# Sparse attention into a split-precision MLP: weight fetches of the first combined chunk, PSUM rotation and the transposition of the probabilities

## The chip, the cores and the metric

The kernel runs on one core of one Trainium2 chip. The metric is the device time of one execution in microseconds. Before the change three runs gave a median of 704.69 us (702.12 to 708.5).

## What is computed

```python
k_sum, v_sum = max and mean of k, v over blocks of 32 keys          # (4, 8, 24, 64)
scores = [q.k/8 where |i-j| < 16 else -1e9,  q.k_sum/8 + log 32]
a = softmax(scores);  attn = a @ [v, v_sum]                         # q, k, v: (4, 8, 768, 64)
x = attn, heads side by side                                        # (3072, 512)
out = ((x @ w_a) * (x @ w_b)) @ w_out      # w_a, w_b: (512, 1536), w_out: (1536, 512)
```

Everything is 32-bit float.

## The kernel before

Each number is held as a high and a low part, and a product is three matmuls (high by high, high by low, low by high). The hidden dimension is cut into 12 blocks of 128, numbered `f`; a block has one tile of `w_a`, one of `w_b` and one of `w_out`, all 36 kept in SBUF (`homes`). The 24 groups of 128 tokens are cut into eight chunks `u`: four chunks of two groups, then from `PLAIN = 4` on four chunks of four groups (512 tokens).

Chunks 0 to 3 use the weights as they are (`item`, matmuls at L1358 and L1429). Chunks 4 to 7 use combined weights (`fast`): seven products of half size instead of eight, from the block's two own tiles (number 0, and half of number 3) and from two sums and differences of them (numbers 1 and 2). `combine` makes these for all 12 blocks while chunks 2 and 3 run: it adds the parts (L1277), subtracts in halves (L1285), splits the results into high and low (L1296 and L1297), and writes all four tiles to a buffer in HBM, `store`, through SP's DMA queue. In `fast` each of 48 items (chunk by block) reads its four tiles back with `fetch` (L1492, `t<-combined` in the profile), into one of two rings of four tiles that alternate. The freed homes of the weights serve as rings, as the chunk's inputs (`XTILES`, two sets) and as gates (`GATES`, the homes of block 11).

An item of `fast` is seven products of six matmuls each (L1522), into the two halves of the PSUM banks `h0` and `h1`; ScalarE copies the first out (L1534) and VectorE adds the others into `acc` in SBUF (L1536, L1539, L1542, L1544). The two results are multiplied on GpSimd (L1550; in chunk 7 on VectorE), cast by ScalarE (L1552), the low part is subtracted on GpSimd (L1555), and twelve matmuls with `w_out` follow (L1562).

Beside all this runs the attention of the chunks to come, one group of 128 tokens at a time. Scores (L855) go to the banks `c0` and `c1`, one for each half of the heads; VectorE scales and masks them (L875) and takes the maximum (L883), ScalarE the exponentials (L912), GpSimd divides (L938). The probabilities are turned by twelve VectorE transpositions per group (L983), each 32 partitions by eight pieces of 32 columns, which place each block directly. Then come the products with the values (L999) in `c0`, and ScalarE copies these to `S0` (L1010). When a chunk's four groups are there, `mix` makes the seven combined inputs: subtractions on VectorE (L1332), high parts on ScalarE (L1327), low parts on GpSimd (L1328). `prep_values` sums blocks of `v` on GpSimd (L778) at a new batch.

Every instruction is put into a list with a rank, and `Work.emit` writes the program. A table `ORDER` gives the order of each of the five engines (SP's is that of the DMA issues) word for word; an engine never leaves that order.

Of the kernel before, what the change touches and what calls it, by code (L numbers as in the profile page):

```python
# [333 lines left out]
def attention_moe(  # L334
# [10 lines left out]
    nc = tc.nc  # L345
# [26 lines left out]
    COPIES = ("AA", "AA", "AA", "AA")  # L372
    MEANS = "DPP"
    TURNS = 5
    FILL = 2

    const = ctx.enter_context(tc.tile_pool(name="const", bufs=1))
    wp = ctx.enter_context(tc.tile_pool(name="weights", bufs=1))
# [1285 lines left out]
```

## Time and profile before

| | before |
|---|---|
| median of three runs | 704.69 us |
| the profiled execution, own time | 701.9 us |
| its span, first to last instruction | 700.2 us |
| granted TensorE clock, mean | 0.978 of full speed |
| busy: TensorE matmul / weight load | 641.7 / 571.7 us |
| busy: VectorE / GpSimd / ScalarE | 498.2 / 361.6 / 252.5 us |
| moved by DMA | 164.92 MB, 236 GB/s on the average |

All durations come from the one profiled execution. Busy times of TensorE include time in which a matmul waits in the array's pipeline, since the ends of matmuls are modelled; how fast it streams is read from stretches in which nothing holds it up. The stages used below are: chunks 0 to 3 up to 267.4 us, then the combined chunks 4, 5, 6 and 7, which start at 267.4, 391.6, 498.9 and 597.5 us with their first matmul at L1522.

### The profile page before, as it was taken

The page shows a single profiled execution, that of the slowest core. Times are in us where ns is not written, and L with a number is a line of the kernel's source. Part 1 is how long each engine was busy: PE and PEld are TensorE (multiplying, and loading weights), DVE is VectorE, ACT ScalarE, POOL GpSimd, SP SyncE. Part 2 cuts the span into 40 slices and gives each one's busy share as a digit, 9 for nine tenths or more (in the row PEclk, how much of TensorE's full clock was granted, in tenths as well). Part 3 has the DMA queues.
Part 4 walks back from the last instruction along what each step waited for, and adds up shares of the span by engine and source line. Part 5 has one row for each costly group of instructions (what it writes and reads, how often), then busy time and mean ns, then how long its engine had stood idle before and what let it go on. Part 6 is the DMA issues. An engine that isn't in the chain of part 4 may idle for free.

```text
span 700.2 us, 14435 instructions
## 1 busy us (share of the span) xinstructions
PE 641.7 (92%) x5316; PEld 571.7 (82%) x5316; DVE 498.2 (71%) x974; ACT 252.5 (36%) x706; POOL 361.6 (52%) x386
## 2 busy tenths in 40 slices
PE   7899999997998988889988989899999999999995
PEld 5699877786987867778877878789899989989995
DVE  4877899975899968636787988688876643444442
ACT  4887866331445423321323401515142121111111
POOL 6773555642678669677357643445635455211110
PEclk9899999999999999999998999999999999999998
DMA  9999944255779888988988887878967867678661
GB/s 248 285 277 277 320 87 96 65 144 151 239 236 310 252 283 256 299 243 266 324 235 239 244 234 233 276 232 258 291 200 267 283 232 252 204 283 300 239 200 60
DMA packets 186911, 164.92 MB, mean 236 GB/s; under 512 B 136264, under 2 KB 148808, under 8 KB 186840
## 3 DMA queue, kind: packets, MB, share of 16 engines
q1 hardware_dynamic: 186696, 163.86, 78.4%
q8 instruction: 42, 0.69, 0.4%
q14 instruction: 29, 0.24, 0.1%
q10 hardware_dynamic: 144, 0.13, 0.1%
HBM read 135.20 MB, written 28.31 MB: 234 GB/s over the span
## 4 chain that ended last, share of the span: by engine, by line
PE 45%; DVE 19%; DMA 17%; POOL 6%; SPq 6%; issue 4%; ACT 2%; DVEq 0%; ACTq 0%; POOLq 0%
PE h L1522 20%; PE o L1562 11%; DMA t<-combined 9%; PE h L1358 6%; SPq L529 5%; DVE pt L983 4%; PE o L1429 3%; DMA S<-in_v_dram 3%; PE c L999 2%; DVE S L1332 2%; DMA combined<-t 2%; POOL S L778 2%; DVE S L1285 2%; DVE c L595 1%; SPq L1492 1%
## 5 line engine op out<-in xcount | busy, mean ns | idle before, releaser
L1522 PEld LDWEIGHTS h<-x,t 128*128 128x128 f32 x2016 | 249.6, 194 | 42.2 <-issue 8.4
L1522 PE MATMUL h<-x,t 128*128 128x256 f32 x2016 | 260.2, 280 | 24.5 <-DMA t<-combined 11.5
L1562 PE MATMUL o<-w,gate 128*128 128x512 f32 x576 | 149.2, 385 | 1.7 <-POOL gate L1555 1.7
L1358 PE MATMUL h<-x,w 128*128 128x256 f32 (+1 forms) x792 | 135.0, 327 | 4.9 <-DVE gh L1420 4.6
L1358 PEld LDWEIGHTS h<-x,w 128*128 128x128 f32 x792 | 118.5, 192 | 17.7 <-DVE gh L1420 6.1
L1562 PEld LDWEIGHTS o<-w,gate 128*128 128x128 f32 x576 | 100.2, 193 | 11.7 <-POOL gate L1555 2.1
L1555 POOL TENSOR_TENSOR gate<-g,gate 128x512 fp32r<-128x512 f32 x47 | 61.0, 1298 | 90.9 <-ACT gate L1552 90.6
L1550 POOL TENSOR_TENSOR g<-sums 128x512 f32<-128x512 f32 x36 | 47.6, 1321 | 89.8 <-DVE sums L1544 78.7
L1536 DVE TENSOR_TENSOR sums<-h,sums 128x512 f32<-128x512 f32 x48 | 33.1, 689 | 77.2 <-PE h L1522 68.2
L1534 ACT COPY sums<-h 128x256 f32<-128x256 f32 x48 | 17.8, 371 | 149.1 <-PE h L1522 129.7
L983 DVE STREAM_TRANSPOSE pt<-s 32x256 f32<-32x256 f32 x144 | 62.7, 435 | 4.4 <-POOL s L938 1.8
L1552 ACT CAST gate<-g 128x512 fp32r<-128x512 f32 x48 | 29.7, 619 | 90.5 <-POOL g L1550 41.6
L1544 DVE TENSOR_TENSOR sums<-h,sums 128x512 f32<-128x512 f32 x48 | 33.0, 688 | 31.5 <-PE h L1522 30.6
L912 ACT ACTIVATE s<-s,nml 128x120 f32<-128x120 f32 x112 | 43.1, 387 | 33.6 <-DVE nml L883 33.5
L778 POOL TENSOR_TENSOR S<-S 96x512 f32<-96x512 f32 (+3 forms) x42 | 32.2, 767 | 29.7 <-DMA S<-in_v_dram 27.8
L1429 PE MATMUL o<-w,last 128*128 128x512 f32 x174 | 43.8, 388 | 0.7 <-ACT last L1417 0.6
L938 POOL TENSOR_TENSOR s<-s,nml 128x480 f32<-128x480 f32 x32 | 32.0, 1008 | 23.3 <-DVE nml L934 16.8
L1328 POOL TENSOR_TENSOR x<-S,x 128x512 fp32r<-128x512 f32 x28 | 37.8, 1356 | 5.1 <-ACT x L1327 4.9
L611 POOL TENSOR_TENSOR w<-S,w 128x512 fp32r<-128x512 f32 x24 | 30.6, 1282 | 18.6 <-ACT w L608 14.6
L1429 PEld LDWEIGHTS o<-w,last 128*128 128x128 f32 x174 | 31.8, 190 | 6.6 <-ACT last L1417 2.3
L1542 DVE TENSOR_TENSOR sums<-h,sums 128x512 f32<-128x512 f32 x48 | 33.0, 687 | 4.4 <-PE h L1522 3.3
L1297 POOL TENSOR_TENSOR t<-S,t 128x512 fp32r<-128x512 f32 x24 | 30.9, 1296 | 7.3 <-ACT t L1296 7.3
(153 smaller groups left out, 863.0 us busy)
## 6 DMA issues: line engine op xcount, KB each, us to landing
t<-combined SPq DMA_DIRECT2D x144, 512.0 KB
combined<-t SPq DMA_DIRECT2D x24, 512.0 KB
t<-combined SPq DMA_DIRECT2D x48, 256.0 KB
raw<-in_moe_w_a_dram SPq DMA_DIRECT2D x12, 512.0 KB
raw<-in_moe_w_b_dram SPq DMA_DIRECT2D x12, 512.0 KB
raw<-in_moe_w_out_dram SPq DMA_DIRECT2D x12, 512.0 KB
combined<-w SPq DMA_DIRECT2D x12, 512.0 KB
out_dram<-S SPq DMA_DIRECT2D x23, 256.0 KB
```

The costliest lines, as they stand in the source:

```text
L529: lambda: nc.sync.dma_start(out=out, in_=in_), rate=rate,
L778: lambda: nc.gpsimd.tensor_tensor(out=out, in0=i0, in1=i1, op=ALU.add),
L912: lambda h=h, c=c, more=more: nc.scalar.activation(y[h][:, c, :], x[h][:, c, :], AF.Exp, bias=m[:, 0, h, c : c + 1], scale=1.0, **more,),
L983: lambda js=js, qs=qs, rs=rs: nc.vector.transpose(out=pv[js, rs, qs], in_=sv[qs, rs, js]),
L1328: pool(rank, 1.24, [f"S0.{i}", hk], [lk], lambda: nc.gpsimd.tensor_tensor(out=half(1), in0=raw(i), in1=half(0).bitcast(F32), op=ALU.subtract))
L1358: nc.tensor.matmul(ps, w[:, c, part, :], xin[xpart][:, :, c].rearrange("p g (a b) -> p g b a", a=2), start=(i == 0), stop=(i == n - 1),)
L1429: nc.tensor.matmul(bank[ok[j]], (gh if first else gl)[:, j * P : (j + 1) * P], w[:, :, part, :].rearrange("p (z a) n -> p z n a", a=2), st ...
L1522: nc.tensor.matmul(ps, w[:, c, part, :], x[:, xpart, c].rearrange("p g (a b) -> p g b a", a=2), start=m == 0, stop=m == 5,)
L1536: dve(CHAIN, 0.65, ["h1", "h1R", rk], [f"{ak}.0", f"{ak}.1"], lambda: nc.vector.tensor_tensor(out=acc(0, 2), in0=h1, in1=acc(5).broadcast_ ...
L1550: lambda eng=nc.gpsimd if slow else nc.vector: eng.tensor_tensor(out=g, in0=acc(0, 5)[:, 0:4:3], in1=acc(0, 5)[:, 2:5:2], op=ALU.mult))
L1555: lambda eng=nc.gpsimd if n < n1 - 1 else nc.vector: eng.tensor_tensor(out=gate(i, 1), in0=gt, in1=gate(i, 0).bitcast(F32), op=ALU.subtract),
L1562: nc.tensor.matmul(bank[f"o{j}"], gate(i, z)[:, j * P : (j + 1) * P], w[:, :, part, :].rearrange("p (z a) n -> p z n a", a=2), start=f == ...
```

## The change

- Blocks 8 to 11 (`HELD`) are no longer combined during chunks 2 and 3. In chunk 4 their own two tiles are read from their homes, and tiles 1 and 2 are made in the ring just before use (`combine(f, r)`); all four are still written to `store` for the later chunks. Chunk 4 takes the blocks in the order 0, 8, 1, 9, 2, 10, 3, 11, 4, 5, 6, 7 (`TURN_OF`).
- Odd chunks take that order backwards, and a chunk's first two items use what the last two of the chunk before left in the rings: no fetch. The tiles change their places: gates go to block 4's homes, the second set of inputs mostly to the held blocks' homes, and tile 3 of both rings shares one home.
- The last two products of an item go to `c1`; which half of `h0` a product takes alternates by item. The sum is written in `c1`, and the multiplication (now on VectorE in all chunks) reads it there.
- Scores of chunks 5 to 7 use `c0` alone: two half steps, one after the other, and the values after them.
- Probabilities from chunk 3 on: one VectorE transposition of all 128 partitions (chunks 3 and 4: two, of half the columns) into a scratch tile, then 12 (24) ScalarE copies of 32 partitions put the blocks where they belong.
- In `mix` the subtractions move from VectorE to GpSimd, but for chunk 4, where they stay on VectorE and everything is done in two halves. In chunk 4's attention a second buffer lets the next group's scores begin before the present group's transposition. Copies of finished outputs (`finish`, to `S1`) go to ScalarE, except for the last chunk's.
- `ORDER` is written anew for all engines.

The diff without the table, cut to its core:

```diff
-        pe(-1, 1.06, [qk] + (near if masked else KT), banks, fn)
+        split = banks[0] == banks[1]
+        if not split:
+            pe(-1, 1.06, [qk] + (near if masked else KT), banks, fn)
         x = [bank[n].rearrange("p (c x) -> p c x", x=P)[:, :, :COLS] for n in banks]
...
+            if split:
+                pe(-1, 0.53, [qk] + KT, banks[:1], lambda h=h: fn((h,)))
...
+        for rows in (slice(0, 8),) if u > PLAIN else (slice(0, 4), slice(4, 8)):
+            n = rows.stop - rows.start
+            tk = ["turn"] if n == 8 else [f"kin0.{r}" for r in range(0, P, 32)]
+
+            def turn_room(n=n):
+                x = kin[:, : 4 * P]
+                if n == 8:
+                    if not turning:
+                        turning.append(wp.tile([P, 8 * P], F32, tag="last", name="turning"))
+                    x = turning[0]
+                return x.rearrange("p (n x) -> p n x", x=P)
+
+            dve(
+                rank, 0.71 if n == 4 else 1.3, sk if n == 8 else [sk[rows.start // 4]], tk,
+                lambda rows=rows, turn_room=turn_room: nc.vector.transpose(out=turn_room(), in_=sv[:, rows, :]),
+            )
+            for i, j in pairs_ij:
+                qs, js = slice(32 * i, 32 * (i + 1)), slice(32 * j, 32 * (j + 1))
+                act(
+                    rank, 0.13 + n * 32 / 1030, tk + ["S0.2"] * own, [f"{key}{i}{j}"],
+                    lambda js=js, qs=qs, rows=rows, turn_room=turn_room: nc.scalar.copy(
+                        out=pv[js, rows, qs], in_=turn_room()[qs, :, js]
+                    ),
+                )
...
-        banks = ["c0", "c1"]
+        banks = ["c0", "c1" if u <= PLAIN else "c0"]
...
-                if i + 1 < n and not after and u > PLAIN:
+                if i + 1 < n and not after:
                     begin(i + 1)
                 bring(i)
                 turned(i)
-                if i + 1 < n and u == PLAIN:
-                    begin(i + 1)
...
     AT = [3 * f + x for f in range(NF) for x in range(2)]
-    XTILES = (AT[:7], AT[15:22])
-    RING = (AT[7:11], AT[11:15])
-    GATES = AT[22:24]
+    HELD = (8, 9, 10, 11)
+    TURN_OF = (0, 8, 1, 9, 2, 10, 3, 11, 4, 5, 6, 7)
+    XTILES = (AT[1:8], AT[17:24])
+    RING = (AT[10:13] + AT[:1], AT[13:16] + AT[:1])
+    GATES = AT[8:10]
     store = dram.tile([NF, 4, P, 1024], I32, name="combined")
...
+        base = 0 if ring is not None else f % 2 * 2
+        first, second_ = f"S1.{base}", f"S1.{base + 1}"
+        rank = MIX + 0.001 * f
+        end = [] if ring is not None else [f"end{f}"]
...
-            (((2, 0), (1, 0), (1, 2)), ALU.add), (((2, 2), (0, 0), (1, 0)), ALU.subtract),
-            (((3, 0), (1, 2), (2, 2)), ALU.subtract), (((3, 2), (0, 2), (3, 0)), ALU.subtract),
+            (((0, 0), (0, 0), (1, 0)), ALU.subtract), (((1, 0), (1, 0), (1, 2)), ALU.add),
+            (((1, 2), (1, 2), (0, 0)), ALU.subtract), (((0, 2), (0, 2), (1, 2)), ALU.subtract),
         ):
-            (pool if o[0] == 3 else dve)(
-                MIX, 0.72 if o[0] == 3 else 0.36, [f"S1.{i}" for i in {x[0], y[0]} - {o[0]}], [f"S1.{o[0]}"],
-                lambda o=o, x=x, y=y, op=op, eng=nc.gpsimd if o[0] == 3 else nc.vector: eng.tensor_tensor(
+            eng = (dve, nc.vector) if o[1] == 0 else (pool, nc.gpsimd)
+            eng[0](
+                rank, 0.78, [f"S1.{base + i}" for i in {x[0], y[0]} - {o[0]}], [f"S1.{base + o[0]}"],
+                lambda o=o, x=x, y=y, op=op, eng=eng[1]: eng.tensor_tensor(
                     out=room(*o, 2), in0=room(*x, 2), in1=room(*y, 2), op=op),
...
+        for j, x, home in ((1, 1, a), (2, 0, b)):
+            i = home if ring is None else RING[ring][j]
+            keys, key = tile_keys(i), f"S1.{base + x}"
...
+        apart = u == PLAIN
+        cuts = [slice(g, g + 1) for g in range(G)] if apart else [slice(0, G)]
...
+        def less(o, x, y, gs):
+            (dve if apart else pool)(
+                rank, 0.78 if apart else 1.31, [named(f"S0.{i}", gs) for i in (x, y) if i != o], [named(f"S0.{o}", gs)],
+                lambda eng=nc.vector if apart else nc.gpsimd: eng.tensor_tensor(
...
-            copy, eng = ((nc.scalar.copy, act), (nc.vector.tensor_copy, dve))[j % 2]
+            copy, eng = ((nc.scalar.copy, act), (nc.vector.tensor_copy, dve))[j % 2 if end or space == "S0" else 0]
...
     ORDERED = (
-        (0, (0, 0), 0, "h0", 0), (1, (0, 1), 1, "h1", 0.1), (5, (2, 0), 5, "h1R", 0.15),
-        (6, (1, 1), 6, "h0R", 0.25), (4, (1, 0), 4, "h0", 0.3), (3, (3, 0), 3, "h1", 0.4),
-        (2, (2, 1), 2, "h1R", 0.45),
+        (0, (0, 0), 0, 0, 0), (1, (0, 1), 1, "h1", 0.1), (5, (1, 1), 5, "h1R", 0.15),
+        (6, (2, 0), 6, 1, 0.25), (4, (1, 0), 4, 0, 0.3), (3, (3, 0), 3, "c1", 0.4),
+        (2, (2, 1), 2, "c1R", 0.45),
     )
...
+        own = ("h0", "h0R") if i == 0 else ("h0R", "h0")
+
+        def product(j, y, k, hk):
+            if u == PLAIN and f in HELD and j in (0, 3):
+                w, y_ = homes[3 * f + j // 3], y + j // 3
+            else:
+                w, y_ = rings[RING[r][j]], y + (j == 3) * r
+            w = w[:, 2 * y_ : 2 * y_ + 2]
             x = x_tile(s, k)
...
-        dve(CHAIN, 0.65, ["h1", "h1R"], [f"{ak}.2", f"{ak}.3"], lambda: nc.vector.tensor_tensor(
-            out=acc(2, 2), in0=h1, in1=acc(2, 2), op=ALU.add))
+        dve(CHAIN, 0.69, [f"{ak}.2", f"{ak}.3"], ["c1", "c1R"], lambda: nc.vector.tensor_tensor(
+            out=c1, in0=c1, in1=acc(2, 2), op=ALU.add))
-        slow = n < n1 - NF
-        (pool if slow else dve)(
-            CHAIN, 1.24 if slow else 0.65, [f"{ak}.{x}" for x in (0, 2, 3, 4)], ["g0", "g1"],
-            lambda eng=nc.gpsimd if slow else nc.vector: eng.tensor_tensor(
-                out=g, in0=acc(0, 5)[:, 0:4:3], in1=acc(0, 5)[:, 2:5:2], op=ALU.mult))
+        dve(CHAIN, 0.69, ["c1", "c1R", f"{ak}.0", f"{ak}.4"], ["g0", "g1"], lambda: nc.vector.tensor_tensor(
+            out=g, in0=c1, in1=acc(0, 5)[:, 0:5:4], op=ALU.mult))
...
-        elif (3 in us) and f < NF:
-            combine(f)
+        elif 3 in us:
+            if f not in HELD:
+                combine(f)
...
-        u, f = PLAIN + (n - n0) // NF, (n - n0) % NF
+        u, z = PLAIN + (n - n0) // NF, (n - n0) % NF
+        f = TURN_OF[NF - 1 - z if u % 2 else z]
+        r = (z + u) % 2
         if n == n0:
             next(attention(u + 1))
-        if f == 0 and u < NU - 1:
+        if z == (8 if u == PLAIN else 0) and u < NU - 1:
             mix(u + 1)
-        if f == 7 and u < NU - 2:
+        if z == (8 if u == PLAIN else 7) and u < NU - 2:
             next(attention(u + 2))
-        fetch(n, f)
-        fast(n, u, f, n0, n1)
+        if u == PLAIN and f in HELD:
+            combine(f, r)
+        elif u == PLAIN or z > 1:
+            fetch(f, r)
+        fast(n, u, z, f, r, n0, n1)
```

## Rows read from the trace of the kernel before

**Rows 1.** Windows by stage: each engine's busy us, then clock, DMA share, GB/s.
```profile
160.00:267.40 107.40, 97.96 (x766) 83.94 (x766) 90.33 (x174) 43.53 (x125) 69.23 (x65) 0.97 0.81 248
267.40:391.60 124.20, 105.86 (x945) 95.05 (x946) 88.12 (x171) 37.01 (x123) 80.86 (x86) 0.95 0.91 266
391.60:498.90 107.30, 98.85 (x900) 89.67 (x898) 89.56 (x190) 32.97 (x115) 55.70 (x53) 1.00 0.86 252
498.90:597.50 98.60, 96.20 (x845) 89.45 (x844) 57.18 (x110) 24.41 (x70) 44.70 (x36) 1.00 0.75 248
```

**Rows 2.** Groups of TensorE instructions by line and shape: count, busy us, mean ns, idle before.
```profile
L1522 PE MATMUL h<-x,t 128*128 128x256 f32 x2016 | 260.2, 280 | 24.5 <-DMA t<-combined 11.5 <-DVE sums L1536 2.6 <-DVE sums L1542 2.1
L1562 PE MATMUL o<-w,gate 128*128 128x512 f32 x576 | 149.2, 385 | 1.7 <-POOL gate L1555 1.7
```

**Rows 3.** Chain that ended last, stretches where TensorE streams: start us, us, what.
```profile
331.73 1.05 PE c L855 x32
...
415.13 1.08 PE c L999 x32
...
548.34 2.59 PE o L1562 x12
...
637.87 3.35 PE h L1522 x30
```

**Rows 4.** The same chain inside the first combined chunk.
```profile
309.97 5.56 DMA S<-in_v_dram
...
335.25 7.00 DMA combined<-t
343.18 8.12 DMA t<-combined
```

**Rows 5.** Timeline of ScalarE at the first combined item.
```profile
288.89 0.62 ACT L1552 CAST gate<-g 128x512 fp32r<-128x512 f32 x1 [1.69 <-DMA combined<-t]
```

**Rows 6.** TensorE's waits from 160 to 267 us: releaser, total us, times, longest.
```profile
PE c L999 <- DMA vw<-S: 4.3, 1, 4.3
PE h L1358 <- DVE gh L1420: 3.8, 2, 2.7
```

**Rows 7.** Groups of VectorE instructions by line and shape.
```profile
L983 DVE STREAM_TRANSPOSE pt<-s 32x256 f32<-32x256 f32 x144 | 62.7, 435 | 4.4 <-POOL s L938 1.8
L1536 DVE TENSOR_TENSOR sums<-h,sums 128x512 f32<-128x512 f32 x48 | 33.1, 689 | 77.2 <-PE h L1522 68.2 <-POOL g L1550 3.5 <-POOL x L1328 2.7
...
L1332 DVE TENSOR_TENSOR S<-S 128x512 f32<-128x512 f32 x16 | 21.9, 1371 | 2.6 <-ACT S L1010 2.3
...
L875 DVE SCALAR_TENSOR_TENSOR s<-c,mask 128x480 f32<-128x480 f32 x28 | 17.7, 646 | 4.9 <-PE c L855 4.6
...
L1277 DVE TENSOR_TENSOR S<-w 128x512 f32<-128x512 f32 x12 | 13.0, 1082 | 0.9 <-POOL S L1285 0.9
...
L740 DVE STREAM_TRANSPOSE kT<-kin 128x576 f32<-128x576 f32 x6 | 4.6, 767 | 0.4 <-DMA kin<-in_k_dram 0.4
```

**Rows 8.** Timeline of VectorE near the end of the first combined chunk.
```profile
376.33 4.21 DVE L1332 TENSOR_TENSOR S<-S 128x512 f32<-128x512 f32 x1
```

**Rows 9.** Timeline of GpSimd over the same instruction: first and last of four.
```profile
376.23 1.27 POOL L1328 TENSOR_TENSOR x<-S,x 128x512 fp32r<-128x512 f32 x1
...
379.95 0.90 POOL L778 TENSOR_TENSOR S<-S 96x128 f32<-96x128 f32 x1
```

**Rows 10.** Groups of ScalarE instructions by line and shape.
```profile
L1534 ACT COPY sums<-h 128x256 f32<-128x256 f32 x48 | 17.8, 371 | 149.1 <-PE h L1522 129.7 <-DVE sums L1544 10.1 <-DVE half L752 8.3
...
L1010 ACT COPY S<-c 128x512 f32<-128x512 f32 x16 | 9.4, 585 | 28.0 <-PE c L999 28.0
```

**Rows 11.** Groups of GpSimd instructions by line and shape.
```profile
L1550 POOL TENSOR_TENSOR g<-sums 128x512 f32<-128x512 f32 x36 | 47.6, 1321 | 89.8 <-DVE sums L1544 78.7 <-DVE nml L928 6.7 <-DVE ksum L761 4.2
```

**Rows 12.** DMA issues by line, the fetches: count, size of each.
```profile
t<-combined SPq DMA_DIRECT2D x144, 512.0 KB
...
t<-combined SPq DMA_DIRECT2D x48, 256.0 KB
```

More of the change, by code (lines that the diff above doesn't have):

```diff
@@ L450, in attention_moe @@
     xt = wp.tile([P, 8, NP, P], F32R, tag="x", name="x")
-    last = sb([P, CV], "last", F32R)
-    gt, gg = sb([P, 2 * CH], "g"), sb([P, 2 * WIDE * P], "gh", F32R)
+    ends = wp.tile([P, CV + 2 * WIDE * P], F32R, tag="last", name="ends")
+    last, turning = ends[:, :CV], []
+    gt, gg = sb([P, 2 * CH], "g"), ends[:, CV:]
     ght, glt = gg[:, : WIDE * P], gg[:, WIDE * P :]
@@ new lines, in transposes, with turned @@
+        if u in BY_PE:
+            for h in range(2):
+                def turned(h=h):
+                    for c in range(NP):
+                        nc.tensor.transpose(
+                            bank[banks[h]][:COLS, c * P : (c + 1) * P], s[h][:, c, :COLS], ident
+                        )
+                pe(-1, 0.53, [sk[h]], [banks[h]], turned)
+                act(
+                    rank, 0.52, [banks[h]] + ["S0.2"] * own, [f"{key}{i}{j}" for i in (2 * h, 2 * h + 1) for j in range(4)],
+                    lambda h=h: nc.scalar.copy(
+                        out=dst[:COLS, h], in_=bank[banks[h]][:COLS].rearrange("p (c x) -> p c x", x=P)
+                    ),
+                )
+            return
@@ L1291, in dest @@
             def dest(i=i):
-                if i not in combined:
-                    combined[i] = tile_of(i)
-                return combined[i]
-            act(MIX, 0.6, [key], keys, lambda j=j, dest=dest: nc.scalar.copy(out=dest()[:, :, 0, :], in_=room(2 + j)))
-            pool(MIX, 1.24, [key, keys[0]], keys[1:], lambda j=j, dest=dest: nc.gpsimd.tensor_tensor(
-                out=dest()[:, :, 1, :], in0=room(2 + j), in1=dest()[:, :, 0, :].bitcast(F32), op=ALU.subtract))
-            work.add("SP", 40, 0.47, 524.0, keys, [f"d{f}.{1 + j}"], lambda j=j, dest=dest: nc.sync.dma_start(
-                out=store[f, 1 + j], in_=dest().bitcast(I32).rearrange("p c z n -> p (c z n)")), rate=300)
+                held = combined if ring is None else rings
@@ new lines, in dest @@
+                if i not in held:
+                    held[i] = tile_of(i)
+                return held[i]
+            act(rank, 0.6, [key], keys, lambda x=x, dest=dest: nc.scalar.copy(out=dest()[:, :, 0, :], in_=room(x)))
+            pool(rank, 1.31, [key, keys[0]], keys[1:], lambda x=x, dest=dest: nc.gpsimd.tensor_tensor(
+                out=dest()[:, :, 1, :], in0=room(x), in1=dest()[:, :, 0, :].bitcast(F32), op=ALU.subtract))
+            work.add("SP", 40, 0.47, 524.0, keys, [f"d{f}.{j}"], lambda j=j, dest=dest: nc.sync.dma_start(
+                out=store[f, j], in_=dest().bitcast(I32).rearrange("p c z n -> p (c z n)")), rate=300)
@@ new lines, in mix @@
+        for gs in cuts:
+            parts_of(0, 0, gs)
+            parts_of(1, 1, gs)
+            parts_of(2, 3, gs)
+            less(0, 2, 0, gs)
+            less(2, 3, 2, gs)
+            less(3, 3, 0, gs)
+            less(1, 1, 3, gs)
+            parts_of(5, 3, gs)
+            parts_of(6, 2, gs)
+            parts_of(4, 0, gs)
+            parts_of(3, 1, gs)
+        if apart:
+            for k in range(7):
+                bridge([f"{x}g{g}" for x in x_keys(s, k) for g in range(G)], x_keys(s, k))
+            for i in range(4):
+                bridge([f"S0.{i}g{g}" for g in range(G)], [f"S0.{i}"])
@@ L1526, in product @@
                     m += 1
-        for _, (j, z), k, hk, off in ORDERED:
-            pe(
-                n + off, 0.672, x_keys(s, k) + tile_keys(RING[i][j]), [hk],
-                lambda j=j, z=z, k=k, hk=hk: product(j, z, k, hk),
+        for _, (j, y), k, hk, off in ORDERED:
+            hk = own[hk] if hk in (0, 1) else hk
+            pe(
+                n + off, 0.672, x_keys(s, k) + (
+                    tile_keys(3 * f + j // 3) if u == PLAIN and f in HELD and j in (0, 3) else ring_keys(r, j)
+                ), [hk],
+                lambda j=j, y=y, k=k, hk=hk: product(j, y, k, hk),
@@ L1560, in down @@
             w = weight(f, "o")
[L1561 removed]
+            for part, y in ((0, 0), (1, 0), (0, 1)):
                 nc.tensor.matmul(
[L1563 removed]
+                    bank[f"o{j}"], gate(i, y)[:, j * P : (j + 1) * P],
                     w[:, :, part, :].rearrange("p (z a) n -> p z n a", a=2),
[L1565 removed]
+                    start=z == 0 and part == 0 and y == 0, stop=z == NF - 1 and y == 1,
                 )
```

146 lines of the change are left out of this document (75 added, 71 removed), and 405 rows, old and new, of the table ORDER.

## Prediction

> **What bounds the kernel now.** I read the windows by stage first, then the groups by line, then the chain that ended last. TensorE is counted busy for 92% of the span, but that overstates it, so I took its pace from stretches of the chain where nothing holds it up: 30 product matmuls in 3.35 us are 0.112 us each, twelve output matmuls take 2.59 us, and a group's scores and values take 1.05 and 1.08 us [rows 3]. The 48 items hold 2016 and 576 of these matmuls, 42 and 12 each [rows 2]. So an item streams in 42 x 0.112 + 2.59 = 7.28 us, twelve in 87.4 us, and a chunk with four attention groups beside it (8.5 us) in 95.9 us. Against that the combined chunks 4, 5 and 6 last 124.2, 107.3 and 98.6 us [rows 1]: 28.3, 11.4 and 2.7 us more. The change can take away only this excess, and what is lost before 267 us; its matmuls stay the same in number and size.
>
> Chunk 4 is where to look. DMA is busy for 0.91 of it, the granted clock is 0.95 of full speed (which stands at 1.00 in chunks 5 and 6), and GpSimd has 80.9 us in it [rows 1]. The chain runs through DMA there: a load of `v`, a store of a combined tile (7.00 us), then a fetch (8.12 us) [rows 4]. Twelve fetches wait their turn among late stores. The first gate is cast at 288.89 us, 21 us after the chunk's first product, after a wait for a store [rows 5]: its tile is block 11's home, which is stored last.
>
> **Part 1: four blocks held, order, places.** A fetch of a block is 3 x 512 + 256 KB = 1.835 MB [rows 12]. Chunk 4 moves 124.2 us x 266 GB/s = 33.0 MB, chunk 5 107.3 x 252 = 27.0 MB [rows 1]. Chunk 5's are 22.0 MB of fetches and 5.0 of attention and output; by that measure chunk 4 has 33.0 - 22.0 - 5.0 = 6.0 MB of stores. After the change it needs 8 fetches (14.7 MB), four blocks of stores (7.3) and the same 5.0: 27.0 MB. At the stage's own 266 GB/s that is 101.5 us, at 266 / 0.91 = 292 GB/s 92.5 us, against 95.9 us of TensorE. DMA thus stops being the sole limit but stays close. The wait for block 11's store goes; next late is `combine` of block 8, wanted by the second item. Its work is not new, three blocks of it come from before 267 us; what it queues is. SP now issues 16 stores within the chunk, those of the sums only after GpSimd's low parts, and behind them in SP's order stand the next fetch and the attention's loads. I price this at nothing while a fetch is asked for an item (7.3 us) ahead, and at up to 8 us, one fetch like that of [rows 4], where it isn't.
>
> I expect chunk 4 at 104 us, near the middle between chunk 6's 98.6 and chunk 5's 107.3, the two that run with the same work beside them and no spilled stores: -20 us. The bounds are -25.6 (as good as chunk 6) and -12 (27.0 MB, delayed by some 10 us of stalls like those above). Chunk 5 loses two fetches of twelve, and waits that Part 2 removes. I take it from 107.3 to 101.3 us, half of its excess and a little more: -6, between 0 and -8.7. In chunks 6 and 7 the fetches are hidden already, so I take nothing.
>
> A rule of the Trainium skill bears on the DMA term: "DMA: Bandwidth & Descriptors", Specifications, gives a limit of about 358 GB/s between HBM and a core. By it the 27.0 MB would take an estimated 75 us, and DMA would be no limit at all; no stage of [rows 1] runs above the 266 of chunk 4, so I keep the rows' rate.
>
> **Part 2: three banks, and the multiplication.** All waits on record of TensorE at the products sum to 24.5 us, of which 11.5 are for fetches; those for VectorE to clear a bank begin with 2.6 and 2.1 [rows 2]. With `c1` the next item's products no longer wait for the last addition. This is inside the terms of Part 1 and is not added again. Moving the multiplication takes 36 x 1.32 us from GpSimd [rows 11] and gives VectorE 36 x 0.69 = 25 us, as one operand is in PSUM like that of L1536 [rows 7]. The chain from sum to gate is 0.6 us shorter per item; the twelve output matmuls come more than an item later, so this is covered.
>
> **Part 3: turning the probabilities.** 18 groups change (240 transpositions by the program, of which one of three rows stands; 24 stay). 216 x 0.435 = 94 us leave VectorE [rows 7]. The new large transposition is not in the trace: 1024 columns at the rate of L740's 576 in 0.767 us are 1.36 us, half of it 0.68, so 12 x 1.36 + 12 x 0.68 = 25 us come back. ScalarE gets 144 copies of 256 columns, 0.371 us each by L1534 [rows 10] or 53 us, and 144 of 128 columns, between half of that and all of it: 27 to 53 us. I take 37. From 252 us it rises to some 345, in stages where it was at most 41% busy after 160 us [rows 1]. It costs nothing as long as no copy waits for its transposition in front of a gate's cast; if it does, the cast is late by up to 12 x 0.371 = 4.5 us, which the item between gate and output matmuls covers.
>
> Before 267 us this helps most: 48 of those transpositions lie in the last 90 us of that stage, where VectorE is busy for 90.3 of 107.4 us [rows 1] and TensorE waits 3.8 us for its result and 4.3 us for batch 1's sums of `v` [rows 6]. The sums have their own chain on GpSimd and DMA, so I take half of the two: -4, between 0 and -8.1.
>
> **Part 4: `mix` and the rest.** Twelve subtractions of 1.371 us leave VectorE [rows 7] for GpSimd, where 512 columns cost 1.32 [rows 11]. That makes mix a chain of eleven GpSimd instructions, 14.5 us, behind it and between them the gates; chunk 5's can only begin after the eighth item, as the held homes must be free. Four items, 29 us, cover it. Copies of finished outputs are eight instructions moved to an engine with room: nothing.
>
> **Sum.** -20 - 6 - 4 = -30 us. The profiled execution (span 700.2, own time 701.9) is 2.8 us below the median, an ordinary run; I take the sum from the median: 704.7 - 30 = 675 us. With the bounds of the terms it is 662 to 693.
>
> **The rivals.** *VectorE is held up by GpSimd.* One subtraction of `mix` took 4.21 us [rows 8] where L1536 takes 0.69, and GpSimd ran four instructions without a gap over that time [rows 9]. The held blocks' combining puts 12 such VectorE instructions beside a busy GpSimd, chunk 4's mix eight. At L1277's mean [rows 7] each costs 0.39 us extra, 8 us in all and hidden; at the 3.5 us of [rows 8] 70 us, and combine is then late for every second item. Chunk 4 then gains 6 us, chunk 5 half of its 6, the stage before nothing: 696 us. The skill's "SBUF — State Buffer" (SBUF: two separate sides) states that GpSimd and a VectorE instruction with two SBUF inputs share a port pair which the first to come holds for its whole instruction. By that each wait would end with one GpSimd instruction, an estimated 26 us for the twenty, and the gain would be nearer the forecast; the row shows a longer wait. Chance 0.15.
>
> *The attention of chunk 5 is late anyway.* Before, its `mix` was at work 15 us before the chunk's end [rows 8], so chunk 4's length may be set not by fetches but by the loads and sums of batch 2's `v` [rows 4], which the change doesn't touch. Chunk 4 then shrinks by 2 us, by what mix saves, and chunk 5 by its 6: 697 us. Against it speaks that these loads stand in the same queue as the fetches that go. Chance 0.12.
>
> *Slower: `c0` alone.* In chunks 5 to 7 scores, scores and values of 12 groups pass through one bank: 36 hand-overs. If TensorE comes to each just behind the one before, it waits for the reader (0.65 us for L875, 0.59 for L1010 [rows 7, 10]) and for an instruction in front of that (0.69): 1.3 x 36 = 47 us, so 675 + 47 = 722 us. From 0.83 us per hand-over on, all of the gain is gone. Against it: values used `c0` alone already, and TensorE's order can put products between. Chance 0.10.
>
> **How the numbers follow.** The forecast has the other 0.63. 658 to 700 us takes in its bounds and both weak-gain rivals, and leaves out the slower one and some of the tails. This kernel's measurement can't tell less than about 1% (7 us) from no change. Faster by more: 0.61 of the forecast, and some 0.14 of the 696 and 697 cases, 0.75. Within 1%: 0.15. Slower: 0.10.
>
> **What the changed profile would show.** If right: chunk 4 takes 100 to 108 us with a clock near 1.00; the first gate comes within 12 us of the first product; L983 has 24 transpositions of the old form; VectorE is near 430 us, ScalarE near 345, GpSimd near 330; DMA moves some 18 MB less (ten fetches). The port rival shows as L1277 and L1332 at 2 us or more, the late attention as chunk 5's first product right behind `mix`, the bank rival as TensorE waiting at L855 for L875 and at L999. Wrong altogether it would be if the new order of TensorE stalls where the trace gives no hint, as no row of before shows that order.

## The result and the profile after

The change makes the kernel faster: 682.12 us, median of four runs (681.87 to 682.62), against 703.43 us for the kernel before in the same series; the ratio is 0.9685, 95% interval 0.9634 to 0.9736. 675 us were predicted, 658 to 700 as the range. So the gain is 21.3 us and not 30. Ratios compare the means of the executions that show no slower state of the chip, so they aren't always the quotient of the medians. The profiled execution of the kernel after took 682.07 us, its span 680.3.

The windows by stage of the kernel after, for [rows 1] (stage and length, then busy us of TensorE, its weight loads, VectorE, ScalarE, GpSimd, then clock, DMA share, GB/s):

```profile
160.00:265.60 105.60, 100.37 (x793) 87.92 (x792) 66.51 (x118) 79.45 (x251) 65.73 (x69) 0.97 0.68 208
265.60:379.10 113.50, 106.09 (x923) 95.97 (x923) 76.89 (x140) 57.11 (x166) 75.14 (x84) 0.97 0.77 213
379.10:478.50 99.40, 99.17 (x881) 92.18 (x880) 66.24 (x131) 51.79 (x150) 39.25 (x40) 1.00 0.82 232
478.50:581.10 102.60, 102.47 (x897) 94.20 (x896) 56.35 (x96) 52.02 (x145) 39.20 (x33) 1.00 0.65 207
581.10:680.30 99.20, 93.13 (x667) 86.74 (x665) 41.59 (x65) 15.67 (x31) 15.36 (x12) 0.99 0.62 207
```

The boundaries are each chunk's first product, found by counting 504 products to a chunk. Counted so, chunks 4 to 7 of the kernel before start at 267.4, 393.1, 499.9 and 597.2 us; [rows 1] put two of them up to 1.5 us early. From stage to stage:

| | start of chunk 4 | chunk 4 | chunk 5 | chunk 6 | chunk 7 | span |
|---|---|---|---|---|---|---|
| before | 267.4 | 125.7 | 106.8 | 97.3 | 103.0 | 700.2 |
| after | 265.6 | 113.5 | 99.4 | 102.6 | 99.2 | 680.3 |
| change | -1.8 | -12.2 | -7.4 | +5.3 | -3.8 | -19.9 |
| forecast | -4 | -20 | -6 | 0 | 0 | -30 |

The chain that ended last in the kernel after, first its shares by engine, and groups of instructions by line and shape, the first two for [rows 2], the third for L855 of the kernel before, and the last ScalarE's new copies:

```profile
PE 75%; DVE 7%; DMA 6%; POOL 4%; ACT 3%; SPq 3%; issue 2%; POOLq 0%; DVEq 0%; ACTq 0%
...
L1613 PE MATMUL h<-x,t 128*128 128x256 f32 x1392 | 184.1, 280 | 6.4 <-ACT t L1361 3.9
L1653 PE MATMUL o<-w,gate 128*128 128x512 f32 x576 | 144.6, 382 | 0.6 <-POOL gate L1646 0.6
L864 PE MATMUL c<-kT,qT 64*64 64x120 f32 x640 | 34.5, 275 | 3.2 <-DVE x L1073 3.2
L1033 ACT COPY pt<-turning 32x256 f32<-32x256 f32 x144 | 58.0, 403 | 7.5 <-DVE turning L1027 4.9
```

TensorE's waits in front of products are 6.4 us in this row and 8.0 with the other rows of L1613 (24.5 before, [rows 2]), and from chunk 5 on there are none above 0.8 us: in chunks 5 and 6, where TensorE is busy for 99.17 of 99.4 and 102.47 of 102.6 us, it is itself the bound. The third row is what I had overlooked. The same 640 score matmuls are counted busy for 34.5 us; before it was this:

```profile
L855 PE MATMUL c<-kT,qT 64*64 64x120 f32 x640 | 22.3, 276 | 4.0 <-DVE qT L1187 3.4 <-DVE S L603 0.5
```

The chain shows why (start, us, what; for the L855 row of [rows 3]):

```profile
377.44 0.97 PE c L864 x16
...
381.91 0.97 PE c L864 x16
...
385.87 0.97 PE c L864 x16
```

Thirty-two scores of both halves of the heads took 1.05 us; sixteen of one half take 0.97. By the kernel's tile positions a half step uses one half of the array's rows and leaves the other idle. A group thus costs 2 x 0.97 - 1.05 = 0.89 us more, twelve groups 10.7 us. Counted by chunk, the score matmuls fall on chunks 4, 5 and 6 as 192, 128 and 64 before and as 160, 112 and 112 after, so scores stream for an estimated 3.4, 2.6 and 4.7 us more in them.

### The profile page after: what moved, and what is told of

It is laid out like the page before. It is cut to its first block, busy times and chain, and to the rows that moved or that the text cites. A ratio compares the mean times of both kernels' runs of the same rounds, so it can differ in the third digit from the quotient of the medians.

```text
span 680.3 us, 14515 instructions
## 1 busy us (share of the span) xinstructions
PE 646.7 (95%) x5316; PEld 581.8 (86%) x5316; DVE 436.3 (64%) x802; ACT 362.7 (53%) x1009; POOL 329.9 (48%) x370
## 4 chain that ended last, share of the span: by engine, by line
PE 75%; DVE 7%; DMA 6%; POOL 4%; ACT 3%; SPq 3%; issue 2%; POOLq 0%; DVEq 0%; ACTq 0%
PE h L1613 25%; PE o L1653 18%; PE c L1613 10%; PE h L1441 9%; PE c L864 4%; PE o L1512 4%; SPq L538 2%; DMA combined<-t 2%; PE c L1049 2%; POOL t L1362 1%; ACT pt L1033 1%; DVE c L604 1%; DMA qin<-in_q_dram 1%; DMA space<-in_k_dram 1%; DVE S L612 1%
## 5 line engine op out<-in xcount | busy, mean ns | idle before, releaser
L1613 PE MATMUL h<-x,t 128*128 128x256 f32 x1392 | 184.1, 280 | 6.4 <-ACT t L1361 3.9
L1613 PEld LDWEIGHTS h<-x,t 128*128 128x128 f32 x1392 | 172.9, 193 | 16.6 <-ACT t L1361 4.3
L1653 PEld LDWEIGHTS o<-w,gate 128*128 128x128 f32 x576 | 100.4, 190 | 12.2 <-issue 1.6
L1613 PE MATMUL c<-x,t 128*128 128x256 f32 x552 | 75.4, 278 | 0.0
L1628 ACT COPY sums<-h 128x256 f32<-128x256 f32 x48 | 17.9, 373 | 107.2 <-PE h L1613 90.6
L1613 PEld LDWEIGHTS c<-x,t 128*128 128x128 f32 x552 | 70.5, 193 | 2.3 <-issue 0.5
L1512 PE MATMUL o<-w,ends 128*128 128x512 f32 x288 | 71.2, 389 | 1.1 <-ACT ends L1500 1.1
L1033 ACT COPY pt<-turning 32x256 f32<-32x256 f32 x144 | 58.0, 403 | 7.5 <-DVE turning L1027 4.9
L1638 DVE TENSOR_TENSOR c<-c,sums 128x512 f32<-128x512 f32 x48 | 33.5, 698 | 44.2 <-PE c L1613 43.2
L1512 PEld LDWEIGHTS o<-w,ends 128*128 128x128 f32 x288 | 53.3, 192 | 9.8 <-ACT ends L1500 2.2
L1400 POOL TENSOR_TENSOR x<-S,x 128x512 fp32r<-128x512 f32 (+1 forms) x35 | 37.2, 1081 | 8.5 <-ACT x L1398 8.5
L1641 DVE TENSOR_TENSOR g<-c,sums 128x512 f32<-128x512 f32 x48 | 33.2, 691 | 9.8 <-POOL gate L1646 6.3
```

Source lines behind the costliest of these rows:

```text
L1033: lambda js=js, qs=qs, rows=rows, turn_room=turn_room: nc.scalar.copy(out=pv[js, rows, qs], in_=turn_room()[qs, :, js]),
L1400: pool(rank, 0.72 if apart else 1.31, [named(f"S0.{i}", gs), hk], [lk], lambda: nc.gpsimd.tensor_tensor(out=half(1), in0=raw(i)[:, :, gs], ...
L1512: nc.tensor.matmul(bank[ok[j]], (gh if first else gl)[:, j * P : (j + 1) * P], w[:, :, part, :].rearrange("p (z a) n -> p z n a", a=2), st ...
L1613: nc.tensor.matmul(ps, w[:, c, part, :], x[:, xpart, c].rearrange("p g (a b) -> p g b a", a=2), start=m == 0, stop=m == 5,)
L1638: dve(CHAIN, 0.69, [f"{ak}.2", f"{ak}.3"], ["c1", "c1R"], lambda: nc.vector.tensor_tensor(out=c1, in0=c1, in1=acc(2, 2), op=ALU.add))
L1641: dve(CHAIN, 0.69, ["c1", "c1R", f"{ak}.0", f"{ak}.4"], ["g0", "g1"], lambda: nc.vector.tensor_tensor(out=g, in0=c1, in1=acc(0, 5)[:, 0:5: ...
```

## Experiments

All medians beside the kernel before on the same chip: first series (four kernels) 704.11 us, second 702.75, third 701.38. The kernel after, run again in the first series, took 682.50 us, ratio 0.9682 [0.9623, 0.9741]; chunk 4 starting at 263.9 us and the chunks lasting 116.4, 99.4, 102.6 and 99.2.

> The changed kernel once more, on the chip on which the next three run, as their measure. Expected: 0.9685 of the time before, as it was measured.

**Half of the scores left out.** In chunks 5 to 7 each half step does 8 of its 16 score matmuls; the rest is left out, and the masked scores of these heads are wrong.

```diff
-            for c in range(NP):
+            for c in range(NP) if len(part) == 2 else range(NP // 2):
```

> Leaves out the second half of the score matmuls in each half step of chunks 5 to 7 (8 of 16; those scores are stale). Theory: with the scores in one bank the two halves of the heads can no longer run beside each other in TensorE; 16 matmuls take 0.97 us where 32 took 1.05, so 12 groups cost 10.7 us more, and as TensorE is busy without a gap in chunks 5 and 6 (99.2 of 99.4 us, 102.5 of 102.6) this is in the time. Taking 24 x 0.48 us = 11.6 us away gives 8 to 12 us back: 671 to 675 where the changed kernel has 682. Rival: TensorE's time there is waiting that is counted as busy, the next wait takes the place: 679 to 683.

674.16 us, ratio 0.9571 [0.951, 0.963]: 8.3 us less than the kernel after, as the theory had it. The chain of this run shows what half of a half step takes:

```profile
379.46 0.56 PE c L864 x8
...
383.01 0.56 PE c L864 x8
```

That is 0.56 us and not 0.48, so 24 x 0.41 = 9.8 us of streaming are gone and not the 11.6 expected. Scores on TensorE are on the path, each us of them worth about 0.85. By that the 10.7 us of the half steps cost an estimated 9 us of time. Against the second run of after, chunks 4 to 6 are 4.1, 2.9 and 2.8 us shorter, and chunk 7, which has no scores, is as long; chunk 4 alone varies by 2.9 us between the two runs of after.

**Block 8's combining earlier.** Finished outputs of chunks 2 and 3 go through `S0` alone, so that `S1` is free sooner, and block 8's combining (`combine`) moves forward in the orders of VectorE, GpSimd and ScalarE.

```diff
-            finish(row0, ok, "S0" if u < FILL else "S1", CHAIN)
+            finish(row0, ok, "S0", CHAIN, both=u < FILL)
```

> The outputs of chunks 2 and 3 are copied to S0 instead of S1, so that S1 is free, and block 8's combining is moved forward in the orders of VectorE, GpSimd and ScalarE, to before the end of chunk 3. Theory: chunk 4's second item waits some 10 us for that combining; it starts at once, and of the 10 us 6 to 10 come off: 672 to 676. Rival 1: the sums of v and the keys of batch 2 that now come 5 us later hold up chunk 5's attention, and chunk 4 ends no earlier: 679 to 684. Rival 2: the wait moves to block 9, 2 to 4 us come off.

687.38 us, ratio 0.9749 [0.969, 0.981], 5 us more than the kernel after: the theory fell, and both rivals' ranges lie below it. The first wait is gone, others stand in its place. TensorE's waits from 265 to 300 us in this run:

```profile
PE h L1573 <- DVE sums L1590: 3.2, 1, 3.2
PE h L1573 <- ACT sums L1588: 2.9, 1, 2.9
PE c L1573 <- DVE g L1601: 2.8, 1, 2.8
```

The cast of block 8's tile now stands in ScalarE's order ahead of the first item's copy, and waits 6.41 us for GpSimd, which is at the sums of `v` for most of that time.

**The 12 VectorE transpositions back, in the kernel after.** Two runs: in chunks 5 to 7 the probabilities are turned as before, by 12 VectorE instructions straight to their places (into two destinations in turn), without ScalarE's copies; first as one piece of 5.2 us in VectorE's order, then as 12 instructions that each stand behind another VectorE instruction.

```diff
-            dve(rank, 1.3, sk, tk, lambda: nc.vector.transpose(out=turn_room(), in_=sv[:, rows, :]))
-            for i, j in pairs_ij:
-                act(rank, 0.38, tk, [f"{key}{i}{j}"], lambda: nc.scalar.copy(...))
+            for i, j in pairs_ij:
+                dve(rank, 0.435, sk, [f"{key}{i}{j}"], lambda: nc.vector.transpose(out=to[js, :, qs], in_=sv[qs, :, js]))
```

> Undoes the turning of the probabilities in chunks 5 to 7: twelve VectorE transpositions straight into the destination, no copies on ScalarE (two destinations in turn; everything else and the orders as in the changed kernel). VectorE gets 12 x 3.9 = 47 us more, about 15 a chunk, ScalarE 58 less. Theory: VectorE goes from 68, 67 and 55 per cent busy in chunks 4 to 6 to some 80, 82 and 69; blocks of 5.2 us in one piece stand in front of the additions that free the banks, and 3 to 10 us are lost: 685 to 692. Rival: neither engine is on the path in these chunks, the part is worth nothing there: 680 to 684.

> The kernel after, with the 12 VectorE transpositions per group of the kernel before in chunks 5 to 7, and no copies on ScalarE, as in the run with them in one piece (722.95 us), but here as 12 separate instructions of 0.435 us of which each stands behind another VectorE instruction of the old order (8 to 14 of these between the first and the last). Theory 1 (it was the block of 5.2 us in VectorE's order that cost 40 us): 686 to 696 us. Theory 2 (VectorE's load itself is too much for this order): 712 to 725 us.

722.95 us, ratio 1.0253 [1.018, 1.033], and 722.57 us, ratio 1.0291 [1.023, 1.036]: 40 us more than the kernel after, more than the whole gain, and no difference between the two forms. The first run's theory (3 to 10 us) was far too low and the second's Theory 2 holds: it isn't the block, it is VectorE's load or the latency of the turning in this order, which these runs don't tell apart. Chunks 4 to 6 of the second run take 127.4, 115.7 and 115.1 us. TensorE's waits there:

```profile
PE c L1041 <- DVE turning L998: 9.8, 5, 3.9
PE c L1041 <- DVE pt L998: 7.8, 3, 4.3
PE c L1609 <- DVE g L1637: 5.0, 5, 1.5
```

**The same part in the kernel before, alone.** Twice: once 8 of the 12 transpositions of each group in chunks 5 to 7 are left out (only those on the diagonal stay, so the values are multiplied with old data); once they are replaced as in the change, one VectorE transposition and 12 ScalarE copies, with all orders but ScalarE's kept.

```diff
+                        if u <= PLAIN or js == qs else None
```

> The kernel before, in which 8 of the 12 VectorE transpositions of each group of chunks 5 to 7 are left out (96 of 0.435 us, 41.8 us; the four on the diagonal stay, so the products with the values read old data). Nothing else is changed, the order neither. Theory: with the fetches shown to matter little, chunks 4 and 5 of the kernel before are long because VectorE, 88 to 90 us busy there, brings the attention and the sums late: each falls by 5 to 10 us, the run to 685 to 695 us. Rival (VectorE's work was hidden too, and only the loads and sums of v for the next batch hold chunk 4): 700 to 704 us.

> The kernel before with one part of the change alone: in chunks 5 to 7 one VectorE transposition of all 128 partitions for a group and 12 ScalarE copies in place of 12 VectorE transpositions. The copies stand in ScalarE's order right behind the transposition, two by two between the instructions that were there; all other orders stay. VectorE loses 46 us, ScalarE gains 58 us. Theory: as the run with 8 of 12 left out, less 0 to 6 us for copies that are late: 686 to 698 us. Rival (the copies hold up ScalarE's exponentials and gate casts in an order not made for them): 702 us or more.

700.51 us, ratio 0.9961 [0.991, 1.001], and 703.74 us, ratio 1.0012 [0.997, 1.005]: no difference, so both theories fell. VectorE's busy time in chunk 4 falls from 89.5 to 76.8 us in the first of them, and the chunk lasts 126.4 us as ever. In the kernel before, the load of these transpositions is hidden as long as all else stays.

**Fetches left out in the kernel before.** Once those of blocks 8 to 11 in chunk 4 (there the last four items of the chunk), once those of the first two items of chunks 5 to 7; the products use what lies in the rings.

```diff
+                if n < n0 + NF and f > 7:
+                    return
```

```diff
+                if n >= n0 + NF and f < 2:
+                    return
```

> The kernel before, in which chunk 4 does not fetch the tiles of blocks 8 to 11: 16 fetches, 7.34 MB, are left out and the products of these four items use what the rings hold (wrong data, same work). All else, the stores among it, is unchanged. Theory: chunk 4 lasted 125.7 us before because its fetches queued with late stores; 7.34 MB less of its 33.4 MB at 266 GB/s frees up to 27.6 us of DMA, of which some 12 us show as time: chunk 4 at 110 to 116 us, the run at 688 to 695 us. Rival (chunk 4 waited for the combining itself and for the late attention of chunk 5, not for the transfers): chunk 4 stays within 3 us of 125.7, the run at 701 to 706 us.

> The kernel before, in which the first two items of chunks 5, 6 and 7 are not fetched: 24 fetches, 11.0 MB, are left out, as the alternating direction does it, and the products of these items use what the rings hold (wrong data, same work). Theory: these fetches were hidden but for some in chunk 5, whose length falls by 2 to 5 us while chunks 6 and 7 stay as they are: 698 to 702 us. Rival 1 (the spared fetches were the main part of what chunk 5 gained, 7.4 us, and gave chunk 7 its 3.7): 690 to 694 us. Rival 2 (all hidden): 703 to 705 us.

699.08 us, ratio 0.9957 [0.993, 0.999], and 702.18 us, ratio 1.0018 [0.998, 1.005]. The first is some 3 to 4 us less, of which 1.5 lie in chunk 4: the theory, 12 us, fell, and the rival holds for the chunk. The second can't be told from the kernel before. Its profiled execution took 708.41 us, the longest of its ten; chunk 5 lasts 110.8 us there, and TensorE's waits for fetches are 4.8 us (4.5 in the kernel before). Whole chunk 4 of the first run, and its last 20 us:

```profile
264.80:388.90 124.10, 105.18 (x953) 94.27 (x954) 90.97 (x172) 38.58 (x131) 81.06 (x87) 0.96 0.73 210
368.90:388.90 20.00, 15.95 (x172) 14.02 (x172) 19.57 (x23) 9.83 (x35) 14.69 (x14) 0.91 0.63 192
```

DMA at 0.73 in place of 0.91, 210 GB/s in place of 267, and the chunk is 1.5 us shorter.

That each of two parts is hidden when it is taken out alone doesn't show that both are. The chains of chunk 4 show one standing in for the other. In the kernel before it goes through the fetch of block 10, then through `mix`:

```profile
359.13 5.98 DMA t<-combined
...
376.41 4.13 DVE S L1332
```

Without the four blocks' fetches it goes through VectorE's transpositions of the probabilities in place of that fetch:

```profile
352.58 0.44 DVE pt L983
...
372.33 4.02 DVE S L1332
```

With 8 of 12 transpositions left out it goes through two fetches:

```profile
362.87 6.47 DMA t<-combined
369.35 5.61 DMA t<-combined
```

The change takes both away at once; no run left out both in the kernel before.

**Scores in both halves of the array again.** The second half of the heads goes to bank `c1`, in a gap between an item's multiplication and the next item's products there. Three runs: the order of after with the scores moved to the nearest such gap; all orders written anew from the end of chunk 3 on, by a search over longest paths through the same instructions, without this edit; and a new order, found in the same way, with it.

```diff
-                pe(-1, 0.53, [qk] + KT, banks[:1], lambda h=h: fn((h,)))
+                pe(-1, 1.06 if h == 0 else 0.0, ..., ["c0"] if h == 0 else [], fn if h == 0 else lambda: None)
...
-                            bank[banks[h]][es, c * P : c * P + COLS], qT[hs, c, es],
+                            bank[("c0", "c1")[h] if split else banks[h]][es, c * P : c * P + COLS], qT[hs, c, es],
```

> The kernel after, its order kept but for the scores of chunks 5 to 7: they take both halves of the array at once, the second half of the heads in bank c1, at the nearest place in TensorE's order where c1 is free, with VectorE's reads of the two banks moved there. Theory (half steps cost 10.7 us): 672 to 677 us. Rival (12 more hand-overs of c1 in an order not made for them take it back): 681 to 690 us.

> The kernel after with the same instructions in another order: from the end of chunk 3 on, the lists of all five engines are written anew, found by a search over longest paths with the scores' half steps put at 0.97 us. Theory: chunk 4's 113.5 us against 95.9 us of streaming are left over because the waits at its start and its late attention stand in a fixed order, so some of the 17 us can be had by order alone: the run at 670 to 678 us (682.1 after). Rival (chunk 4 is held by the chain of combining and loads that no order changes): 680 to 685 us.

> As the run with the new order, but the scores of chunks 5 to 7 take both halves of the array at once again, as before the change: the second half of the heads goes to bank c1 in the gaps between an item's multiplication and the next item's products there; the order is found in the same way. Theory (half steps cost 24 x 0.97 against 12 x 1.05 us on a TensorE without slack, 10.7 us): 7 to 11 us less than the run with the new order alone. Rival (c1 is needed by the items, and the hand-overs there take the gain back): no less than that run.

In the old order 683.58 us, ratio 0.9736 [0.967, 0.980]: nothing gained, the rival holds. TensorE's waits in chunks 5 and 6 rise from 0.2 us to 6.7, of which 3.2 are for the bank:

```profile
PE c L1586 <- DVE s L861: 1.6, 2, 0.8
PE c L1586 <- DVE sums L861: 1.6, 2, 0.8
```

The new order alone is 691.29 us, ratio 0.9840 [0.979, 0.989], worse than that of the kernel after: its theory fell. With both halves it is 671.22 us, ratio 0.9574 [0.952, 0.963]: 20 us less than the same search without the edit, and less than the kernel after by 11 us in the medians, by 8 in the two ratios. That is the fastest of all. The 20 us are not the edit's alone: it saves 10.7 us of streaming, and the two orders, each found for its own program, differ in more than the scores. Chunks 4 to 6 of it, in windows:

```profile
264.50:371.10 106.60, 96.79 (x908) 87.99 (x907) 74.88 (x138) 54.64 (x156) 71.28 (x81) 0.95 0.79 221
371.10:470.90 99.80, 97.96 (x907) 90.71 (x905) 67.86 (x135) 56.31 (x169) 42.44 (x43) 1.00 0.80 235
470.90:569.00 98.10, 96.98 (x875) 90.11 (x874) 52.82 (x93) 49.01 (x137) 37.04 (x32) 1.00 0.69 220
```

## Why the prediction was right, and where it was not

The sign and the range were right; the forecast of 675 us was 7 us too low. Two steps were wrong: chunk 4's term was made from megabytes, and the scores in one bank were priced without their streaming. The second alone, an estimated 9 us, is about as large as the 8.7 us by which the gain fell short. That the rest of the sum then fits is in part luck, since the run with fewer megabytes doesn't bear out the reasoning under chunk 4's term.

**Chunk 4: -20 forecast, -12.2 measured, and not by the megabytes.** I took its length for one set by DMA (0.91 busy, a chain through fetches and stores) and made the term from the amount moved. With 7.34 MB less DMA was at 0.73 and the chunk 1.5 us shorter. What changed is how long TensorE waits: 18.8 us in chunk 4 before, 7.2 after, by the sum of all rows of its waits. The longest (releaser, total us, times, longest), before and then after:

```profile
PE h L1522 <- DMA t<-combined: 6.2, 4, 3.0
PE c L855 <- DVE qT L1187: 2.8, 1, 2.8
PE h L1522 <- DVE sums L1536: 2.6, 3, 1.5
```

```profile
PE h L1613 <- ACT t L1361: 3.9, 1, 3.9
PE c L1613 <- DVE g L1641: 1.5, 1, 1.5
```

Of the 18.8 us, 6.2 are for fetches and 7.7 for VectorE; after, none is for a fetch and 2.1 are for VectorE. So fetches that come late were waited for, though leaving some out didn't help. Against the 11.6 us less stand 3.4 us more of scores. The chain of the kernel before goes mostly through loads and sums of `v` up to the chunk's first values [rows 4], then through stores and fetches up to 365 us, and at the end through `mix` on VectorE up to 390 us. From 289 us on, the chain of the kernel after is TensorE itself, but for about 1 us. Times from the chunk's start, in us:

| | first values | last values | end of chunk | last values to end |
|---|---|---|---|---|
| before | 60.7 | 105.6 | 125.7 | 20.1 |
| before, blocks 8 to 11 not fetched | 62.8 | 104.1 | 124.2 | 20.0 |
| before, 8 of 12 transpositions left out | 64.2 | 104.8 | 126.4 | 21.5 |
| after | 58.6 | 100.7 | 113.5 | 12.7 |
| after, second run | 61.6 | 103.7 | 116.4 | 12.7 |
| after, block 8 earlier | 64.2 | 106.3 | 119.1 | 12.7 |
| after, transpositions back as one piece | 65.6 | 112.9 | 125.6 | 12.7 |
| after, new order alone | 62.3 | 100.7 | 116.5 | 15.8 |
| both halves of the scores, new order | 55.9 | 96.9 | 106.6 | 9.7 |

7.4 of the 12.2 us lie behind the last values, 2.7 between the first and the last, 2.1 before. The first run without fetches keeps the 20 us at the end, with DMA at 0.63 there. The windows of that stretch, of the kernel before and then of the kernel after:

```profile
373.00:393.10 20.10, 15.85 (x172) 13.99 (x172) 19.78 (x23) 9.85 (x35) 14.80 (x14) 0.92 0.78 254
```

```profile
366.40:379.10 12.70, 12.70 (x129) 11.36 (x129) 6.05 (x12) 5.89 (x16) 11.58 (x11) 1.00 0.14 32
```

Before, VectorE is occupied for 19.78 of 20.1 us, with two subtractions of `mix` at 4.21 us [rows 8] and 4.00 us beside a busy GpSimd, and TensorE waits 4.3 us for the transposition of `q` and for the addition that stand behind them. The other 3 us of the 7.4 are work: TensorE does 172 matmuls in this stretch before and 129 after. After, GpSimd does these subtractions:

```profile
368.22 1.28 POOL L1406 TENSOR_TENSOR S<-S 128x512 f32<-128x512 f32 x1 [0.49 <-ACT S L1061]
...
371.92 4.01 POOL L1406 TENSOR_TENSOR S<-S 128x512 f32<-128x512 f32 x3
```

Three of these take 4.01 us, VectorE is half idle, and TensorE streams all of the 12.70 us at a clock of 1.00. So the row that I quoted for a rival against the change, [rows 8], was a part of the gain, which Part 4 priced at nothing. That the move of `mix` is the cause of it is read from these rows; no run moved it alone, and the run with the new order alone, which moves it too, has 15.8 us there. The rival of the late attention had the first part of the chain right, the loads and sums of `v`. But TensorE waits for nothing in front of chunk 5's first product, in either kernel, and the change did more than that rival's 2 us. The 2.1 us before the first values are within what this point varies by between runs (60.7 to 64.2 in variants of before, 61.6 in the second run of after).

VectorE beside GpSimd was no trouble in the held blocks' combining, the place where I had feared it. Groups of VectorE by line in the kernel after, for L1277 of [rows 7]:

```profile
L1339 DVE TENSOR_TENSOR S<-w 128x512 f32<-128x512 f32 x12 | 13.6, 1140 | 7.6 <-DMA vw<-S 4.6 <-issue 2.5 <-POOL t L1362 0.5
```

1.14 us each is 0.45 more than L1536's 0.69 [rows 7], 5.4 us in all; the longest took 1.77 us. The Trainium skill, "SBUF — State Buffer" (SBUF: two separate sides), has such a VectorE instruction wait for the one GpSimd instruction that holds the shared ports. These 12 agree with it, since none is longer by more than one GpSimd instruction of 1.27 us; the 4.21 and 4.00 us of `mix` in the kernel before, beside several GpSimd instructions, do not.

The first gate is cast 8.4 us after the chunk's first product (21 before, [rows 5]; within 12 was forecast), ScalarE in the kernel after:

```profile
274.01 0.62 ACT L1643 CAST gate<-g 128x512 fp32r<-128x512 f32 x1 [0.78 <-DVE g L1641]
```

The wait for block 11's store is gone, as said. The chunk's length of 100 to 108 us and a clock near 1.00 did not come (113.5 us, 0.97). The late step that I named ("next late is combine of block 8, wanted by the second item") came, but it was not the stores of combined tiles that made it so, and its price of nothing was wrong. GpSimd, VectorE, ScalarE and TensorE in the kernel after:

```profile
278.06 1.26 POOL L1339 TENSOR_TENSOR S<-w 128x512 f32<-128x512 f32 x1 [0.77 <-DMA out_dram<-S]
```

```profile
278.62 1.25 DVE L1339 TENSOR_TENSOR S<-w 128x512 f32<-128x512 f32 x1 [2.54 <-issue]
```

```profile
281.74 0.62 ACT L1361 CAST t<-S 128x512 fp32r<-128x512 f32 x1 [7.11 <-POOL S L1348]
```

```profile
282.41 0.80 PE L1613 MATMUL h<-x,t 128*128 128x256 f32 x2 [3.95 <-ACT t L1361]
283.79 3.78 PE L1613 MATMUL h<-x,t 128*128 128x256 f32 x16 [0.58 <-POOL t L1362]
```

Block 8 can be added only when its room `S1` is free of the outputs of chunk 3, then passes through VectorE, GpSimd and ScalarE in turn. TensorE waits 3.95 us, and the 16 products behind take 0.24 us each in place of 0.112. The run with block 8 earlier didn't gain by taking this wait away. The chunk moved 113.5 us x 213 GB/s = 24.2 MB where 27.0 were forecast.

**"Its matmuls stay the same in number and size."** True, but not the same in time: with scores in one bank, half of the array's rows is idle. This is the term that was missing, 10.7 us of streaming. In the rival of `c0` alone I priced the waits at its hand-overs (47 us), and not the matmuls themselves; all waits of TensorE in chunks 5 and 6 of the kernel after come to 0.2 us. Leaving out half of the scores gives back 8.3 us. Doing them in both halves again gives nothing in an order not made for it; with a new order it comes to the 671.22 us above.

**Chunk 5: -6 forecast, -7.4 measured**, in spite of 2.6 us more of scores. TensorE's waits there fall from 8.2 to 0.2 us; 4.5 of the 8.2 were for fetches. The run that spared fetches alone still waits 4.8 us for others, so it isn't their number by itself. What is left is that they are asked for at another time in the new order; that is argued, not shown. **Chunks 6 and 7: 0 forecast, +1.5 together.** Chunk 6 has 4.7 us more of scores and nine output matmuls more, and waits of 2.3 us before that are gone; chunk 7 has twelve output matmuls less, an estimated 2.6 us at the 0.216 us of [rows 3]. **The start: -4 forecast, -1.8 measured**, within its bounds, but also within what this point varies by: 264.8 and 270.5 us in the two runs on the kernel before that change nothing ahead of it. VectorE is much lighter there (66.5 us in 105.6, 90.3 in 107.4 before) and the time hardly moves.

**The turning of the probabilities.** The forecast took a gain from it only ahead of chunk 4, and saw no cost on ScalarE. The first agrees with the runs on the kernel before, where the later groups' turning alone gives nothing. But it didn't say that the new order stands on it: taken out, the kernel is 40 us slower. VectorE now also does the multiplications, and TensorE waits for its turning and its multiplications in the second of those runs. Why the same part of VectorE's work (485.1 us busy in the first of them, 436.3 in the kernel after) costs 40 us here and nothing in the kernel before is not shown. The engines' busy times came near the forecast: VectorE 436 us (430), ScalarE 363 (345), GpSimd 330 (330); DMA moves 18.4 MB less (18).

What stays open: how much of chunk 4's middle part comes from the second buffer, what `mix` on GpSimd and the third bank for products are worth by themselves, and what fetches and transpositions give when both are left out of the kernel before. None of these was tried. The stores of chunk 4 weren't taken out either.

## What to carry to other kernels

A stage that is 0.9 busy with DMA need not be set by the amount moved: leave some transfers out and look, before costing a change in megabytes. If that shows nothing, read the chain of that run too: other work may have taken the place of what was left out. Look at what the slow instructions of a stage's last stretch wait for. And where a change moves matmuls of a part of the array, price them by how many run side by side, not by their number.

## What was unexpected in the hardware

- Sixteen 64 x 64 matmuls that use one half of the rows take 0.97 us and eight 0.56 us; thirty-two that use both take 1.05 us, and 0.98 us in the run with both halves again.
- After a stretch of 8.8 us at the start of chunk 4 in which TensorE was busy for 3.63 us, its wait of 3.95 us in it, the granted clock is 0.55 for the next 5.2 us, near the lower of its two levels, 1.2 of 2.4 GHz, and 1.00 in the 5 us behind. Windows of the kernel after:

```profile
275.00:283.80 8.80, 3.63 (x15) 2.33 (x13) 6.14 (x16) 1.24 (x2) 6.22 (x10) 0.88 1.03 240
283.80:289.00 5.20, 5.20 (x26) 5.20 (x27) 3.63 (x6) 0.00 (x0) 2.62 (x3) 0.55 1.07 177
289.00:294.00 5.00, 5.00 (x58) 4.44 (x58) 3.11 (x6) 0.89 (x2) 4.12 (x8) 1.00 0.78 268
```

- A ScalarE copy of 32 partitions by 256 columns in SBUF takes 403 ns, no less than one of 128 partitions by 256 columns from PSUM (373 ns, L1628).
